# Load tiles of a cached attention kernel: fixed slots for K and V in place of a rotation of three

## The chip, the cores and the metric

The kernel runs on one core of a Trainium2 chip. The metric is device time in microseconds (us), the median over several executions. "Before" is the kernel as it was, "after" the changed one. Engines in the profile: PE is TensorE, PEld its weight loads, DVE is VectorE, ACT is ScalarE, SP is SyncE, and a q behind a name is that engine's sequencer, which issues the DMAs here. DMAs are the transfers that bring data from HBM, the memory in which the inputs lie, into the tiles on the core; the profile counts 16 DMA engines.

## The reference

Two independent attention blocks A and B are computed and their outputs set side by side. Each has 8 sequences of one token, 32 heads, a cache of 4096 keys and values of 128 elements, all in bfloat16.

```python
q = (x @ wq).reshape(B, Sq, H, Dh).transpose(0, 2, 1, 3)     # x: 8 x 1 x 1024
scores = einsum("bhqd,bhkd->bhqk", q, k_cache) * Dh ** -0.5  # k_cache: 8 x 32 x 4096 x 128
p = softmax(scores)
o = einsum("bhqk,bhkd->bhqd", p, v_cache)
out = o.transpose(0, 2, 1, 3).reshape(B, Sq, H * Dh) @ wo    # per block; the two are concatenated
```

Every byte of K and V is used once, so the kernel has to read 1.1 GB and does little with each byte.

## The kernel before

The caches are cut into 64 K tiles and 64 V tiles, each 8 heads of one sequence: 128 partitions of 64 KB, 8.39 MB. Three such tiles fit. They live in `ring`, in three slots taken in turn by everything that is loaded: wq, K, V, wo and the last part of wo (wo8).

```python
order = [("wq", 0), ("k", 0)]
for n in range(NQ):                      # NQ = 64
    if n == 0:
        order += [("wq", c) for c in range(1, NC)]
    if n + 1 < NQ:
        order.append(("k", n + 1))
    for c in range(NC):
        if n == done_at(c, NC, HB, B) + 1:   # n = 32 and 56
            order.append(("wo", c))
            late[n] = c
    if n == NQ - 1:
        order.append(("wo8", 0))
    order.append(("v", n))
pos = {kn: i for i, kn in enumerate(order)}

def tile_of(kind, n):
    return ring[:, pos[(kind, n)] % NSLOT, :]        # NSLOT = 3

def load_tiles():
    while issued[0] < len(order):
        i = issued[0]
        dep = op_xT if i == 2 else None
        if i >= NSLOT:
            dep = opUse.get(order[i - NSLOT])        # last use of the slot's tenant
            if dep is None:
                return
        ...                                          # one DMA, issued by SyncE behind dep
```

In the rotation V(n) takes the slot of K(n), and K(n+2), which comes next, that of V(n-1). The work on a K tile goes in 8 chunks: VectorE multiplies by q (L299), folds once (L304), TensorE adds up (L313), VectorE reduces (L321). `opUse[("k", n)]` is the TensorE step of the last chunk, `opUse[("v", n)]` the end of PV(n), the product with V(n). PV(n) is done in two halves of 32 matmuls, at chunks 5 and 6 of K tile n+1.

Of the kernel before, what the change touches and what calls it, by code (L numbers as in the profile page):

```python
# [31 lines left out]
class _Program:  # L32
# [9 lines left out]
    def add(self, eng, emit, deps=(), dma_key=None):  # L42
        op = _Op(eng, emit, list(deps), dma_key)
        if dma_key is not None:
            self.counts[dma_key] = self.counts.get(dma_key, 0) + 16
            op.token = (dma_key, self.counts[dma_key])
        for d in op.deps:
            if not (d.eng == "pe" and eng == "pe"):
                d.sig = True
        self.ops[eng].append(op)  # L50
        return op
# [38 lines left out]
def _build_kernel(nc, caches, out):  # L90
    B, Sq, D = caches[0][0].shape
    _, H, Sk, Dh = caches[0][1].shape
    NC = len(caches)
# [6 lines left out]
    CT = 32  # L100
    NR = T // CT
    HB = H // HQ
    NB = NC * HB
    NQ = NB * B
    NS = NQ * NR
    NSLOT = 3
    RG = T // 4 // 4
# [6 lines left out]
    with es:  # L114
# [4 lines left out]
        ring = sb("ring", [128, NSLOT, T * Dh], BF16)  # L119
# [31 lines left out]
        misc_bf16 = misc.bitcast(BF16)  # L151

        sems = {e: es.enter_context(nc.semaphore(f"c_{e}")) for e in ENGINES[1:]}
        for name, n in (("t", NSLOT), ("kl", 2), ("vl", 4), ("x", 1), ("out", 1)):
            for i in range(n):
                sems[(name, i)] = es.enter_context(nc.semaphore(f"{name}{i}"))

# [3 lines left out]
        def dma(out_ap, in_ap, key, deps, eng="sp"):  # L161
            return add(eng, lambda e: e.dma_start(out_ap, in_ap), deps, dma_key=key)  # L162
# [31 lines left out]
        outs = []  # L194


        order = [("wq", 0), ("k", 0)]
        late = {}
        for n in range(NQ):
            if n == 0:  # L200
                order += [("wq", c) for c in range(1, NC)]
            if n + 1 < NQ:
                order.append(("k", n + 1))

            for c in range(NC):
                if n == done_at(c, NC, HB, B) + 1:
                    order.append(("wo", c))
                    late[n] = c
            if n == NQ - 1:
                order.append(("wo8", 0))  # L210
            order.append(("v", n))
        pos = {kn: i for i, kn in enumerate(order)}
        issued = [0]

        def tile_of(kind, n):
            return ring[:, pos[(kind, n)] % NSLOT, :]

        def wo_rows(c):
            return MB * (HB if c < NC - 1 else HB - 1)

        def load_tiles():
            while issued[0] < len(order):
                i = issued[0]
                dep = op_xT if i == 2 else None
                if i >= NSLOT:
                    dep = opUse.get(order[i - NSLOT])
                    if dep is None:
                        return
                kind, n = order[i]
                to = tile_of(kind, n)  # L230
                key = ("t", i % NSLOT)
                if kind in ("k", "v"):
                    blk, b = divmod(n, B)
                    c, hb = divmod(blk, HB)
                    from_ = caches[c][1 if kind == "k" else 2][b, hb * HQ:(hb + 1) * HQ].rearrange("u (m t) d -> (u m) (t d)", m=MP)
                    cuts = [0, NR]
                    if n == NQ - 1:
                        cuts = [0, NR // 2, NR] if kind == "k" else [0, NR // 2, 3 * NR // 4, 7 * NR // 8, NR]
                    for g in range(len(cuts) - 1):
                        cols = slice(cuts[g] * CT * Dh, cuts[g + 1] * CT * Dh)  # L240
                        op = dma(to[:, cols], from_[:, cols], key if len(cuts) == 2 else (kind + "l", g), [dep])
                        for r in range(cuts[g], cuts[g + 1]):
                            opT[(kind, n, r)] = op
                elif kind == "wq":
                    opT[(kind, n)] = dma(to[:, 0:DC * H * Dh], caches[n][3].rearrange("(p k) n -> p (k n)", k=DC), key, [dep])
                elif kind == "wo":
                    rows = wo_rows(n)
                    opT[(kind, n)] = dma(to[0:rows, 0:H * D], caches[n][4][0:rows * H, :].rearrange("(p r) n -> p (r n)", r=H),
                                         key, [dep])
                else:  # L250
                    opT[(kind, n)] = dma(to[:, 0:HQ * D].rearrange("p (j n) -> p j n", j=HQ),
                                         caches[-1][4][(H - HQ) * Dh:, :].rearrange("(j p) n -> p j n", p=128), key, [dep])
                issued[0] += 1
# [91 lines left out]
        def make_pv(n, g0, g1):  # L345
            v = tile_of("v", n)

            def emit(e):
                for g in range(g0, g1):
                    for q in range(4):  # L350
                        t = 4 * (4 * g + q)
                        i = e.matmul(pv_ps[32 * q:32 * (q + 1), :], PM[:, t:t + 4, :].rearrange("p t j -> p (t j)"),  # L352
                                     v[:, t * Dh:(t + 4) * Dh], start=(g == 0), stop=(g == RG - 1), tile_position=(0, 32 * q))
                return i
            op = add("pe", emit, [opExp[n], opT[("v", n, g1 * NR // RG - 1)]] + _at(opAcc, n - 1, []))
            if g1 == RG:
                opPV[n] = opUse[("v", n)] = op

        def make_acc(n):
            opAcc[n] = [add("act", lambda e: e.activation(accS[:], pv_ps[:], ACTF.Copy), [opPV[n], _at(opExt, n - 1)])]  # L360
# [67 lines left out]

        def make_proj_last(norm):
            w = tile_of("wo8", 0)  # L430
            alone = ("wo", NC - 1) not in pos

            def emit(e):
                for j in range(HQ):
                    for q in range(NT):
                        x = e.matmul(proj[32 * q:32 * q + B, 0:DT], on8[:, j, :], w[:, j * D + q * DT:j * D + (q + 1) * DT],
                                     start=(alone and j == 0), stop=(j == HQ - 1), tile_position=(0, 32 * q))
                return x
            make_out(NC - 1, add("pe", emit, [norm, opT[("wo8", 0)], c_proj] + outs))
# [9 lines left out]
        one = sb("one", [128, 1], FP32)  # L449
        c_ones = one[:, 0:1]  # L450
        c_one = add("dve", lambda e: e.memset(one[:], 1.0))
        op_x = [dma(x_sb[:, c, :], caches[c][0].rearrange("b s d -> b (s d)"), ("x", 0), []) for c in range(NC)]

        def emit_xT(e):
            for c in range(NC):
# [2 lines left out]
                    i = e.transpose(misc_bf16[:, col:col + B], x_sb[:, c, :].rearrange("b (p k) -> b k p", k=DC)[:, k, :],  # L458
                                    ident[0:B, 0:B])
            return i  # L460
        op_xT = add("pe", emit_xT, [c_ident, op_x[-1]])
        load_tiles()
        c_xT = last["misc"] = add("dve", lambda e: e.tensor_copy(xT[:], misc_bf16[:, 0:NC * DC * B]), [op_xT])
        for hb in range(HB):
# [10 lines left out]
        for s in range(NS):  # L475
            n, r = divmod(s, NR)
            make_mul(s)
            if s >= 1:
                make_red(s - 1)
            if r == 0 and n >= 1:  # L480
                make_shift(n - 1)
            fold = make_fold(s)
            for k in range(4):
                v = pv_at.get(divmod(s - k, NR))
                if v is None:
                    continue

                k += v in late
                if k == 1 and v in late:
                    make_pv(v, 0, RG // 2)  # L490
                if k < 2:
                    make_pv(v, k * RG // 2, (k + 1) * RG // 2)
                if k == 1:
                    make_acc(v)
                if k == 2:
                    make_ext(v)
                if k == 3:
                    for c in range(NC):
                        if v == done_at(c, NC, HB, B):
                            make_norm(c)  # L500
            if r == 0 and n >= 1:
                make_exp(n - 1)
            if r == 2 and n % B == 0 and n >= 1:
                make_lsum(n // B - 1)

            if n == 0 and r >= 5:
                for i, (hb, f) in enumerate((hb, f) for hb in range(HB) for f in range(2)):
                    if i % 3 == r - 5:
                        for c in range(1, NC):
                            make_q(c, hb, f)  # L510
            c, hb = divmod(n // B, HB)
            if r == 2 and n % B == B - 1 and c + 1 < NC:
                make_qs(c + 1, hb, 0)
                make_qs(c + 1, hb, 1)
            if r == 3 and n + 1 < NQ:
                make_qbc(n + 1)
            if r >= 5 and n - 1 in late:
                i = r - 5
                make_proj(late[n - 1], i * H // 3, (i + 1) * H // 3)
            make_eacc(s, fold)  # L520
            load_tiles()


# [10 lines left out]
            on8[:].rearrange("p j b -> p b j"), o8_ps[:, 0:64].rearrange("p (b j) -> p b j", b=B),  # L534
            rl8[:].rearrange("p (b j) -> p b j", b=B), ALU.mult), [opLsum["rl"], opExt[n]])
        make_proj_last(norm)
        assert issued[0] == len(order)

        counts = P.tokens()
        for o in op_x:  # L540
# [57 lines left out]
```

## Time and profile before

| | before |
|---|---|
| time, median of 4 | 2636.54 us (2633.14 to 2640.33) |
| read from HBM | 1107.33 MB |
| rate over the span | 420 GB/s |
| load queue's packet time, share of 16 engines' span | 98.8% |
| VectorE busy | 80% |

The page's own lines on the queues, before (packets, MB, share of 16 engines; then the total):

```profile
q1 hardware_dynamic: 20688, 1107.35, 98.8%
HBM read 1107.33 MB, written 0.03 MB: 420 GB/s over the span
```

The windows view, before, in long stretches. The columns are the stretch, its length, busy time and instructions of each engine, the granted TensorE clock, the DMA share and GB/s:

```profile
500.00:1000.00 500.00, 244.25 (x1557) 72.57 (x1556) 413.42 (x356) 134.08 (x232) 0.00 (x0) 0.59 1.00 426
1500.00:2000.00 500.00, 244.06 (x1574) 73.12 (x1572) 415.68 (x358) 129.63 (x224) 0.00 (x0) 0.60 1.00 428
```

The last two columns show a share of 1.00 and a steady 426 to 428 GB/s (427 from 41 to 2287 us).

The timeline of the SyncE queue and, below it, of the VectorE steps that waited for a K tile, before (start, length, what; in brackets the idle time before it):

```profile
512.34 0.33 SPq L162 DMA_DIRECT2D ring<-in_A_v_cache_dram  x1
512.71 0.43 SPq L162 DMA_DIRECT2D ring<-in_A_k_cache_dram  x1
550.59 0.33 SPq L162 DMA_DIRECT2D ring<-in_A_v_cache_dram  x1
550.96 0.43 SPq L162 DMA_DIRECT2D ring<-in_A_k_cache_dram  x1
...
515.80 2.29 DVE L299 TENSOR_TENSOR ring<-ring,qbc 128x4096 bf16<-128x4096 bf16 x1 [5.44 <-DMA ring<-in_A_k_cache_dram]
555.29 2.29 DVE L299 TENSOR_TENSOR ring<-ring,qbc 128x4096 bf16<-128x4096 bf16 x1 [6.68 <-DMA ring<-in_A_k_cache_dram]
```

V and K are issued as a pair, and 3.5 us (512.34 to 515.80) and 4.7 us before VectorE starts on the K tile that is still in flight. One pair takes 555.29 - 515.80 = 39.5 us.

The waits view of the SyncE queue from 500 to 1000 us, before: it always waits for the score matmuls on K (13 pairs in 500 us).

```profile
SPq L162 <- PE red L313: 498.7, 13, 39.5
```

The DMA view, before: issues of each kind and the median us from issue to landing.

```profile
ring<-in_A_k_cache_dram SPq DMA_DIRECT2D x32, 43.3
ring<-in_A_v_cache_dram SPq DMA_DIRECT2D x32, 24.2
ring<-in_B_wo_dram SPq DMA_DIRECT2D x1, 33.0
```

And the end of the run, before, in windows of 4 us:

```profile
2592.00:2596.00 4.00, 3.96 (x34) 1.41 (x35) 1.45 (x1) 0.00 (x0) 0.00 (x0) 0.51 1.01 391
2596.00:2600.00 4.00, 3.74 (x44) 1.48 (x42) 3.19 (x3) 0.60 (x1) 0.00 (x0) 1.00 0.09 32
2600.00:2604.00 4.00, 1.37 (x4) 0.41 (x4) 2.57 (x3) 0.00 (x0) 0.00 (x0) 0.85 0.00 0
2604.00:2608.00 4.00, 0.41 (x1) 0.00 (x0) 1.79 (x5) 1.59 (x3) 0.00 (x0) 0.50 0.76 262
```

The last V is to take the last K's slot, so nothing is loaded while VectorE finishes that K. The chain of waits, before, ends with that load (start, us, what):

```profile
2605.77 20.62 DMA ring<-in_B_v_cache_dram
2626.43 1.07 PE pv L352 x8
```

### The profile page before, as it was taken

To read this page: it belongs to the slowest core of one execution; us is meant where nothing else is said; L and a number is where in the kernel's file an instruction comes from. 1 tells how busy PE (TensorE), PEld (TensorE's weight loads), DVE (VectorE), ACT (ScalarE), POOL (GpSimd) and SP (SyncE) were. 2 spreads that over 40 slices of the span, in tenths; PEclk is the share of its full clock that TensorE was granted. 3 is DMA by queue.
4 is the path that set the end of the run, shared out by engine and by line. 5 is a ranking of instruction groups with operands and counts; after the bars stand their busy time and mean duration, and the time that the engine had idled before them with its cause. 6 is when DMAs were issued, how large, how long until landed. Compare 5 with 4: busy or idle time off the path is not lost.

```text
span 2633.7 us, 19575 instructions
## 1 busy us (share of the span) xinstructions
PE 1256.2 (48%) x8130; PEld 380.7 (14%) x8130; DVE 2100.2 (80%) x1807; ACT 675.4 (26%) x1169; POOL 5.7 (0%) x23
## 2 busy tenths in 40 slices
PE   4554454454454454454453544544544544533454
PEld 1111111111111111111111111111111111111111
DVE  3788788888888888788885888888887887858885
ACT  0223223223223223223312232232232232213223
POOL 0000000000000000000000000000000000000000
PEclk8665665665665665665666656656656656665665
DMA  9999999999999999999999999999999999999997
GB/s 415 430 430 426 428 420 429 429 429 424 415 433 425 428 429 416 427 430 421 430 428 429 432 418 434 431 425 430 432 429 427 418 428 430 420 330 431 428 421 303
DMA packets 20840, 1108.61 MB, mean 421 GB/s; under 512 B 2272, under 2 KB 2336, under 8 KB 3376
## 3 DMA queue, kind: packets, MB, share of 16 engines
q1 hardware_dynamic: 20688, 1107.35, 98.8%
q8 instruction: 63, 1.03, 0.1%
q14 instruction: 25, 0.20, 0.0%
q10 hardware_dynamic: 64, 0.02, 0.0%
HBM read 1107.33 MB, written 0.03 MB: 420 GB/s over the span
## 4 chain that ended last, share of the span: by engine, by line
DMA 55%; DVE 36%; PE 6%; ACT 1%; issue 1%; SPq 0%; DVEq 0%
DMA ring<-in_A_k_cache_dram 26%; DMA ring<-in_B_k_cache_dram 25%; DVE ring L299 19%; DVE ring L304 10%; DVE s_sb L321 5%; PE red L313 4%; PE pv L352 2%; DMA ring<-in_B_v_cache_dram 2%; DMA ring<-in_B_wo_dram 1%; ACT PM L340 1%; DMA ring<-in_A_wq_dram 1%; PE q L263 1%; DVE rmax L327 1%; SPq L162 0%; DVE rtmp L329 0%
## 5 line engine op out<-in xcount | busy, mean ns | idle before, releaser
L299 DVE TENSOR_TENSOR ring<-ring,qbc 128x4096 bf16<-128x4096 bf16 x512 | 1170.1, 2285 | 464.8 <-DMA ring<-in_A_k_cache_dram 234.8
L313 PE MATMUL red<-ring,ident 128*128 128x512 bf16 x2048 | 845.8, 559 | 1293.7 <-DVE ring L304 1290.9
L340 ACT ACTIVATE PM<-s_sb,bias,own_sc 128x256 bf16<-128x256 f32 x512 | 609.3, 1607 | 894.6 <-DVE bias L333 894.6
L304 DVE TENSOR_TENSOR ring<-ring 128x2048 bf16<-128x2048 bf16 x512 | 622.0, 1215 | 0.0
L313 PEld LDWEIGHTS red<-ring,ident 128*128 128x128 bf16 x2048 | 203.8, 121 | 1840.7 <-DVE ring L304 1567.5
L321 DVE TENSOR_REDUCE s_sb<-red 128x32 f32<-128x512 f32 x512 | 349.9, 683 | 30.8 <-PE red L313 30.6
L352 PE MATMUL pv<-ring,PM 128*32 128x512 bf16 x4096 | 326.4, 475 | 21.1 <-DMA ring<-in_B_v_cache_dram 21.1
L360 ACT ACTIVATE accS<-pv 128x512 bf16<-128x512 f32 x64 | 38.2, 597 | 885.9 <-PE pv L352 885.9
L340 ACT ACTIVATION_READ_ACCUMULATOR PM<-s_sb,bias,own_sc 128x1 f32 x512 | 255.6, 499 | 0.0
L352 PEld LDWEIGHTS pv<-ring,PM 128*32 128x32 bf16 x4096 | 115.0, 115 | 239.0 <-issue 186.0
L289 ACT ACTIVATE qbc<-misc 128x128 bf16<-128x128 f32 x64 | 17.8, 277 | 138.5 <-PE misc L284 138.5
L263 PE MATMUL q<-ring,xT 128*8 128x512 bf16 x128 | 25.9, 411 | 19.6 <-DMA ring<-in_A_wq_dram 19.6
L373 PE MATMUL o<-accS,E 128*32 128x32 bf16 x896 | 31.7, 177 | 0.0
L373 PEld LDWEIGHTS o<-accS,E 128*32 128x32 bf16 x896 | 25.9, 94 | 24.2 <-ACT accS L360 14.0
L327 DVE TENSOR_REDUCE rmax<-s_sb 128x1 f32<-128x256 f32 x64 | 26.9, 420 | 2.2
L284 PE MATMUL misc<-q_sb,selb 8*32 8x128 bf16 x512 | 26.2, 295 | 0.8 <-ACT q_sb L272 0.8
L272 ACT ACTIVATE q_sb<-q 8x512 bf16<-8x512 f32 x16 | 9.3, 604 | 32.9 <-PE q L263 32.8
L329 DVE TENSOR_SCALAR rtmp<-half,rmax 128x32 f32<-128x32 f32 x64 | 15.4, 241 | 2.3
L284 PEld LDWEIGHTS misc<-q_sb,selb 8*32 8x32 bf16 x512 | 9.2, 103 | 53.9 <-issue 53.9
L333 DVE SCALAR_TENSOR_TENSOR bias<-own_sc,ngm,own_b 128x8 f32<-128x8 f32 x64 | 14.5, 226 | 2.3
L391 PE MATMUL o<-rsum,own_m 128*32 128x8 f32 x112 | 7.2, 202 | 18.2 <-ACT PM L340 18.2
L332 DVE TRANSPOSE_TENSOR_REDUCE ngm<-rtmp 128x1 f32<-128x32 f32 x64 | 13.5, 211 | 2.2
(37 smaller groups left out, 57.7 us busy)
## 6 DMA issues: line engine op xcount, KB each, us to landing
ring<-in_B_k_cache_dram SPq DMA_DIRECT2D x2, 4096.0 KB, 38.0
ring<-in_B_v_cache_dram SPq DMA_DIRECT2D x1, 4096.0 KB, 12.1
ring<-in_B_wo_dram SPq DMA_DIRECT2D x1, 2048.0 KB, 29.0
ring<-in_B_v_cache_dram SPq DMA_DIRECT2D x1, 2048.0 KB, 16.6
ring<-in_B_v_cache_dram SPq DMA_DIRECT2D x2, 1024.0 KB, 19.6
ring<-in_A_k_cache_dram SPq DMA_DIRECT2D x32, 43.3
ring<-in_A_v_cache_dram SPq DMA_DIRECT2D x32, 24.2
ring<-in_B_k_cache_dram SPq DMA_DIRECT2D x31, 43.3
```

Source lines behind the costliest of these rows:

```text
L263: i = e.matmul(q_ps[f][rows, :], xT[:, (c * DC + k) * B:(c * DC + k + 1) * B], w[:, col:col + 512], start=(k == 0), stop=(k == DC - 1), ti ...
L284: x = e.matmul(misc[32 * g:32 * (g + 1), 0:Dh], selb[rows, b, i, :], q_sb[rows, j * Dh:(j + 1) * Dh], start=(i == 0), stop=(i == 1), tile_ ...
L289: "act", lambda e: e.activation(qbc[:, n % 2, :], misc[:, 0:Dh], ACTF.Copy),
L299: opMul[s] = add("dve", lambda e: e.tensor_tensor(v, v, qbc[:, n % 2, :].unsqueeze(1).to_broadcast([128, CT, Dh]), ALU.mult), [opT[("k", n ...
L304: return add("dve", lambda e: e.tensor_tensor(v[:, :, 0:64], v[:, :, 0:64], v[:, :, 64:128], ALU.add), [opMul[s]])
L313: i = e.matmul(dst, ident[:], v[:, :, j, :], start=(j == 0), stop=(j == 3))
L321: opRed[s] = add("dve", lambda e: e.tensor_reduce(s_sb[:, n % 2, r * CT:(r + 1) * CT], red_ps[s % 2][:, :].rearrange("p (t w) -> p t w", w ...
L327: opRmax[n] = add("dve", lambda e: e.tensor_reduce(rmax[:], s_sb[:, n % 2, :], AX.X, ALU.max), [opRed[NR * n + NR - 1]])
L340: return e.activation(PM[:, :, j], s_sb[:, n % 2, :], ACTF.Exp, bias=bias[:, n % 2, j:j + 1], scale=own_sc[:, j:j + 1], accum_out=rsum[:, ...
L352: i = e.matmul(pv_ps[32 * q:32 * (q + 1), :], PM[:, t:t + 4, :].rearrange("p t j -> p (t j)"), v[:, t * Dh:(t + 4) * Dh], start=(g == 0), ...
L360: opAcc[n] = [add("act", lambda e: e.activation(accS[:], pv_ps[:], ACTF.Copy), [opPV[n], _at(opExt, n - 1)])]
L373: x = e.matmul(o_ps[MB * hb:MB * (hb + 1), H * b:H * (b + 1)], E[:, i, PH - 1 - u:PH - 1 - u + MB], accS[:, i * 128 + H * u:i * 128 + H * ...
```

## The change

K tiles take slots 0 and 1 in turn, V always takes slot 2, so V(n) waits for PV(n-1) and K(n+2) for K(n). PV is done in one block of 64 matmuls at chunk 5. x is loaded from ScalarE's queue. Half of the last V goes into a K slot ahead of wo8, the rest behind it.

```diff
-        order = [("wq", 0), ("k", 0)]
+        def put(kind, n, where=None, cuts=None):
+            if where is None:
+                where = kslot[0]
+                kslot[0] = 1 - where
+            slot[(kind, n)] = where
+            plan.append((kind, n, cuts))
+        put("wq", 0, 1)
+        put("k", 0)
+        put("wq", 1, 2)
+        for n in range(NQ - 1):
+            if n + 2 < NQ:
+                put("k", n + 1)
+            else:
+                put("k", n + 1, cuts=((0, NR // 2), (NR // 2, NR)))
             for c in range(NC):
                 if n == done_at(c, NC, HB, B) + 1:
-                    order.append(("wo", c))
+                    put("wo", c)
                     late[n] = c
-            if n == NQ - 1:
-                order.append(("wo8", 0))
-            order.append(("v", n))
+            put("v", n, 2)
+        put("v", NQ - 1, cuts=((0, NR // 2),))
+        put("wo8", 0, 2)
+        plan.append(("v", NQ - 1, ((NR // 2, 3 * NR // 4), (3 * NR // 4, 7 * NR // 8), (7 * NR // 8, NR))))
... # tile_of and load_tiles go by slot[] and by the slot's tenant before
-        op_x = [dma(x_sb[:, c, :], ..., ("x", 0), []) for c in range(NC)]
+        op_x = [dma(x_sb[:, c, :], ..., ("x", 0), [], "act") for c in range(NC)]
... # PV of tile v, at chunk 5 + k of the next K tile
-                if k < 2:
-                    make_pv(v, k * RG // 2, (k + 1) * RG // 2)
-                if k == 1:
-                    make_acc(v)
+                if k == 0:
+                    make_pv(v, 0, RG)
+                    make_acc(v)
```

More of the change, by code (lines that the diff above doesn't have):

```diff
@@ L153, in _build_kernel @@
         sems = {e: es.enter_context(nc.semaphore(f"c_{e}")) for e in ENGINES[1:]}
-        for name, n in (("t", NSLOT), ("kl", 2), ("vl", 4), ("x", 1), ("out", 1)):
+        for name, n in (("t", NSLOT), ("kl", NR), ("vl", NR), ("x", 1), ("out", 1)):
             for i in range(n):
@@ L194, in _build_kernel @@
         outs = []
-        order = [("wq", 0), ("k", 0)]
+        plan = []
+        slot = {}
         late = {}
-        for n in range(NQ):
-            if n == 0:
-                order += [("wq", c) for c in range(1, NC)]
-            if n + 1 < NQ:
-                order.append(("k", n + 1))
+        kslot = [0]
+        def put(kind, n, where=None, cuts=None):
[12 more added lines that the diff above has]
+                put("k", n + 1, cuts=((0, NR // 2), (NR // 2, NR)))
             for c in range(NC):
                 if n == done_at(c, NC, HB, B) + 1:
-                    order.append(("wo", c))
+                    put("wo", c)
                     late[n] = c
-            if n == NQ - 1:
-                order.append(("wo8", 0))
-            order.append(("v", n))
-        pos = {kn: i for i, kn in enumerate(order)}
+            put("v", n, 2)
+        put("v", NQ - 1, cuts=((0, NR // 2),))
+        put("wo8", 0, 2)
+        plan.append(("v", NQ - 1, ((NR // 2, 3 * NR // 4), (3 * NR // 4, 7 * NR // 8), (7 * NR // 8, NR))))
+        tenant = [None, None, ("x", 0)]
+        before = []
+        for kind, n, cuts in plan:
+            w = slot[(kind, n)]
+            before.append(tenant[w])
+            tenant[w] = (kind, n)
         issued = [0]
         def tile_of(kind, n):
-            return ring[:, pos[(kind, n)] % NSLOT, :]
+            return ring[:, slot[(kind, n)], :]
         def wo_rows(c):
@@ L221, in load_tiles @@
         def load_tiles():
-            while issued[0] < len(order):
-                i = issued[0]
-                dep = op_xT if i == 2 else None
-                if i >= NSLOT:
-                    dep = opUse.get(order[i - NSLOT])
+            while issued[0] < len(plan):
+                kind, n, cuts = plan[issued[0]]
+                prev = before[issued[0]]
+                dep = None
+                if prev not in (None, (kind, n)):
+                    dep = opUse.get(prev)
                     if dep is None:
                         return
-                kind, n = order[i]
                 to = tile_of(kind, n)
-                key = ("t", i % NSLOT)
+                key = ("t", slot[(kind, n)])
                 if kind in ("k", "v"):
@@ L235, in load_tiles @@
                     from_ = caches[c][1 if kind == "k" else 2][b, hb * HQ:(hb + 1) * HQ].rearrange("u (m t) d -> (u m) (t d)", m=MP)
-                    cuts = [0, NR]
-                    if n == NQ - 1:
-                        cuts = [0, NR // 2, NR] if kind == "k" else [0, NR // 2, 3 * NR // 4, 7 * NR // 8, NR]
-                    for g in range(len(cuts) - 1):
-                        cols = slice(cuts[g] * CT * Dh, cuts[g + 1] * CT * Dh)
-                        op = dma(to[:, cols], from_[:, cols], key if len(cuts) == 2 else (kind + "l", g), [dep])
-                        for r in range(cuts[g], cuts[g + 1]):
+                    for r0, r1 in cuts or ((0, NR),):
+                        cols = slice(r0 * CT * Dh, r1 * CT * Dh)
+                        op = dma(to[:, cols], from_[:, cols], (kind + "l", r0) if cuts else key, [dep])
+                        for r in range(r0, r1):
                             opT[(kind, n, r)] = op
@@ L430, in make_proj_last @@
             w = tile_of("wo8", 0)
-            alone = ("wo", NC - 1) not in pos
+            alone = ("wo", NC - 1) not in slot
             def emit(e):
@@ L451, in _build_kernel @@
         c_one = add("dve", lambda e: e.memset(one[:], 1.0))
-        op_x = [dma(x_sb[:, c, :], caches[c][0].rearrange("b s d -> b (s d)"), ("x", 0), []) for c in range(NC)]
+        op_x = [dma(x_sb[:, c, :], caches[c][0].rearrange("b s d -> b (s d)"), ("x", 0), [], "act") for c in range(NC)]
         def emit_xT(e):
@@ L460, in emit_xT @@
             return i
-        op_xT = add("pe", emit_xT, [c_ident, op_x[-1]])
+        op_xT = opUse[("x", 0)] = add("pe", emit_xT, [c_ident, op_x[-1]])
         load_tiles()
@@ L482, in _build_kernel @@
             fold = make_fold(s)
-            for k in range(4):
+            for k in range(3):
                 v = pv_at.get(divmod(s - k, NR))
@@ L486, in _build_kernel @@
                     continue
-                k += v in late
-                if k == 1 and v in late:
-                    make_pv(v, 0, RG // 2)
-                if k < 2:
-                    make_pv(v, k * RG // 2, (k + 1) * RG // 2)
+                if k == 0:
+                    make_pv(v, 0, RG)
+                    make_acc(v)
                 if k == 1:
-                    make_acc(v)
+                    make_ext(v)
                 if k == 2:
-                    make_ext(v)
-                if k == 3:
                     for c in range(NC):
@@ L536, in _build_kernel @@
         make_proj_last(norm)
-        assert issued[0] == len(order)
+        assert issued[0] == len(plan)
         counts = P.tokens()
```

## The prediction

> **What bounds it now.** The DMA engines. The page gives the load queue 98.8% of the 16 engines' span and 1107.33 MB read at 420 GB/s, against 80% for VectorE. In the windows view the stretch 41 to 2287 us runs at 427 GB/s, DMA share 1.00. The Trainium skill (HBM Reference, section Access) states about 425 GB/s for a core streaming alone; this trace agrees. One tile (8.39 MB) costs 19.7 us, a K+V pair 39.4 us. VectorE needs about 33.5 us per K tile (8 x (2.29+0.60+1.13) plus 1.2), so it waits for K: 465 us over 63 waits.
>
> Three places aren't at full rate. (a) B's wo load (96 partitions): 33.0 us for 6.3 MB, about 18 us over its share. The change keeps this transfer. (b) The last V: the timeline issues it at 2604.4, when the last K is used, because it rotates into that slot; the 4 us windows show DMA at 32, 0 and 262 GB/s from 2596 to 2608, a hole of 9 to 10 us. It lands at 2626.4. (c) The start: two x issues (0.37+0.28 us) precede the first weight load at 1.56 us.
>
> **What the change does.**
> - Steady state: today V(n) and K(n+2) are issued together when K(n) is used, about 4 us before the tile in flight lands (K's 43.3 us from issue to landing minus 39.4). After, V(n) is issued when PV(n-1) ends, some 13 us before the queue would run dry, and K some 20 us before. With the share already 1.00 this hides little: 0 to 8 us, central 2.
> - PV in one block of 64 matmuls (3.5 us for the first 32, about 6 us together): VectorE waits about 2 us more per tile, inside the 5 to 7 us that it waits for DMA anyhow. No cost until the tail.
> - x on ScalarE's queue: minus 0.7 us. The skill (DMA: Bandwidth & Descriptors, section Issuing engines are not separate DMA queues) says this saves issue time only.
> - Tail: half of the last V goes into K62's slot behind V62, then wo8, then the rest; the hole closes and the last V lands about 2616. But the last K's score work doesn't move: VectorE runs without a gap from 2533.6 on, the exponentials end at 2615.9 today and 2 us later with the longer PV block. The whole last PV (6 us) follows, ending near 2623.5 instead of 2627.5. Of 10 us gained by DMA about 4 reach the end: the bound passes to VectorE and ScalarE.
>
> Sum: 0.7 + 4 + 2, about 7 us (0.25%). **Predicted 2630 us, 2618 to 2637 (8 in 10).** Chances: faster by over 2% 0.01, within 2% 0.98, slower 0.01.
>
> **What would show it.** Mid-run windows still at 425 to 430 GB/s; K's median issue to landing up from 43.3 to about 60 us, V's from 24.2 to about 30 (queued longer, not slower); SyncE's waits split between score matmuls and PV; no DMA hole before the end; the chain of waits in the tail through VectorE and the exponentials, not the last V load; the 330 GB/s slice at B's wo stays.
>
> **What would make it wrong.** If the 16 engines finish a tile unevenly, the shallow queue lets fast ones idle and 427 GB/s isn't the ceiling: a deeper queue could give 15 to 20 us. If V comes later than chunk 5 of the next tile, the longer PV block holds score work, and VectorE could become the bound. If B's wo load was slow because of its neighbours, its 18 us could change too.

## The result, and the profile after

| | before | after |
|---|---|---|
| median of 4 | 2636.54 us | 2604.84 us (2603.57 to 2605.85) |
| ratio | | 0.9879 (95% interval 0.9862 to 0.9896) |
| rate over the span | 420 GB/s | 425 GB/s |
| load queue's share | 98.8% | 99.1% |

Here and below a ratio is the mean time of one kernel's runs over that of the other's of the same rounds, so not quite the ratio of the medians quoted. 31.7 us is clear of noise and over four times the 7 us predicted.

The page's queue lines, after:

```profile
q1 hardware_dynamic: 20656, 1107.32, 99.1%
HBM read 1107.33 MB, written 0.03 MB: 425 GB/s over the span
```

The windows view, after, in the same stretches as before:

```profile
500.00:1000.00 500.00, 239.19 (x1529) 72.80 (x1526) 420.39 (x361) 137.33 (x238) 0.00 (x0) 0.60 1.00 433
1500.00:2000.00 500.00, 248.34 (x1588) 75.54 (x1586) 421.04 (x361) 135.21 (x234) 0.00 (x0) 0.60 1.00 433
```

The DMA share still reads 1.00, and the rate is 433 GB/s in place of 426 to 428. So at a share of 1.00 the engines were not moving all they could.

The timeline of the SyncE queue and of VectorE's waits for K, after:

```profile
500.15 0.33 SPq L162 DMA_DIRECT2D ring<-in_A_v_cache_dram  x1
508.84 0.33 SPq L162 DMA_DIRECT2D ring<-in_A_k_cache_dram  x1
538.29 0.33 SPq L162 DMA_DIRECT2D ring<-in_A_v_cache_dram  x1
546.98 0.33 SPq L162 DMA_DIRECT2D ring<-in_A_k_cache_dram  x1
...
510.61 2.29 DVE L315 TENSOR_TENSOR ring<-ring,qbc 128x4096 bf16<-128x4096 bf16 x1 [3.74 <-DMA ring<-in_A_k_cache_dram]
549.32 2.29 DVE L315 TENSOR_TENSOR ring<-ring,qbc 128x4096 bf16<-128x4096 bf16 x1 [4.31 <-DMA ring<-in_A_k_cache_dram]
```

V is now issued 10.5 us (500.15 to 510.61) before VectorE starts on the K in flight, and K apart from it. A pair takes 549.32 - 510.61 = 38.7 us, 0.8 us less than the pair shown of before. The waits of the SyncE queue from 500 to 1000 us are now split:

```profile
SPq L162 <- PE pv L368: 389.6, 13, 32.5
SPq L162 <- PE red L329: 106.7, 13, 8.3
```

The DMA view, after: V is queued 6 us longer, K is not.

```profile
ring<-in_A_k_cache_dram SPq DMA_DIRECT2D x32, 41.3
ring<-in_A_v_cache_dram SPq DMA_DIRECT2D x32, 30.3
ring<-in_B_wo_dram SPq DMA_DIRECT2D x1, 32.6
```

The tail, after, in windows of 4 us: no window before the last V has landed is empty.

```profile
2568.00:2572.00 4.00, 4.00 (x54) 1.72 (x47) 0.97 (x1) 0.19 (x1) 0.00 (x0) 0.73 1.01 430
2572.00:2576.00 4.00, 1.86 (x12) 0.68 (x10) 3.23 (x3) 0.41 (x1) 0.00 (x0) 1.00 0.79 286
2576.00:2580.00 4.00, 1.41 (x4) 0.43 (x4) 2.53 (x3) 0.00 (x0) 0.00 (x0) 0.62 1.10 412
```

The chain of waits at the end, after: the exponentials and the whole last PV, no longer a load.

```profile
2582.48 9.46 ACT PM L356 x16
2592.67 5.96 PE pv L368 x54
```

**Where the time came from.** In the profiled runs (2633.7 and 2604.0 us) B's wo has landed at 2337.5 before and 2313.1 after, so 24.4 of the 29.7 us were gained by then, in the steady part. From the arrival of the last K but one to the end it took 100.1 us before (from 2533.6) and 96.3 us after (from 2507.65): the tail gave 3.8 us.

The trace also holds every DMA packet. In the steady part a packet is one row of 64 KB, and the usual one takes 2.418 us; 16 engines at that pace move 16 x 65536 B / 2.418 us = 433.6 GB/s. I went through the packets from 34 to 2229 us of the run, and for each V issue counted the bytes issued but not yet moved ("queued", in us at 433.6 GB/s; median and range are over the V issues ahead of tile 32). The third row is what the packets took beyond 2.418 us each; those over 2.45 us alone make up 24.1 us of it before and 4.0 us after:

```
                              before     after
packets in the stretch         14283     14453
packets over 2.45 us            1344       177
time over 2.418 us, per engine  25.5 us    6.9 us
engines idle, per engine        11.8 us    4.8 us
sum lost                        37.3 us   11.7 us
queued at V's issue, median      2.1 us    8.0 us   (before 0.5 to 3.9, after 6.2 to 9.6)
```

The difference of the sums, 25.6 us, is the gain of the steady part: the 170 packets that after moves more in the same stretch are worth 25.7 us at 2.418 us on 16 engines. The table says where the time went, not yet why. A slow packet counts as busy time, which is why the share read 1.00 throughout. Before, the loss follows the data queued when V was issued (slow packets plus idle engines, us per issue, over the issues in that stretch, less the one or two just behind wo): 1.70 below 0.5 us queued (1 issue), 0.93 at 0.5 to 1.5 us queued (12 issues), 0.61 at 1.5 to 2.5 (19), 0.18 at 2.5 to 3.5 (16), 0.07 at 3.5 to 5 (4). After, with 5 to 12 us queued, it is 0.05 to 0.06 (53 issues). A second count, over the 10 us from each issue on, gives 1.96, 0.96, 0.66, 0.18, 0.07 and 0.06 for the same classes.

### The profile page after: what moved, and what is told of

It reads as the page before. It is cut to its first block, busy times and chain, and to the rows that moved or that the text cites. A ratio compares the mean times of both kernels' runs of the same rounds, so it can differ in the third digit from the quotient of the medians. Undisturbed runs are those within 1.5% of the kernel's fastest.

```text
span 2604.0 us, 19575 instructions
## 1 busy us (share of the span) xinstructions
PE 1256.4 (48%) x8130; PEld 387.1 (15%) x8130; DVE 2103.5 (81%) x1807; ACT 675.6 (26%) x1169; POOL 5.7 (0%) x23
## 3 DMA queue, kind: packets, MB, share of 16 engines
q1 hardware_dynamic: 20656, 1107.32, 99.1%
## 4 chain that ended last, share of the span: by engine, by line
DMA 53%; DVE 32%; PE 13%; ACT 2%; issue 1%; DVEq 0%
DMA ring<-in_A_k_cache_dram 26%; DMA ring<-in_B_k_cache_dram 24%; DVE ring L315 16%; DVE ring L320 10%; PE pv L368 6%; PE red L329 6%; DVE s_sb L337 5%; ACT PM L356 1%; DMA ring<-in_B_wo_dram 1%; DMA ring<-in_B_v_cache_dram 1%; DMA ring<-in_A_wq_dram 1%; PE q L279 1%; DVE rmax L343 1%; DVE rtmp L345 0%; DVE bias L349 0%
## 5 line engine op out<-in xcount | busy, mean ns | idle before, releaser
L337 DVE TENSOR_REDUCE s_sb<-red 128x32 f32<-128x512 f32 x512 | 350.2, 684 | 126.1 <-PE red L329 126.1
L368 PE MATMUL pv<-ring,PM 128*32 128x512 bf16 x4096 | 318.0, 479 | 16.6 <-DMA ring<-in_B_v_cache_dram 16.6
L368 PEld LDWEIGHTS pv<-ring,PM 128*32 128x32 bf16 x4096 | 121.5, 118 | 233.7 <-issue 178.8
L389 PE MATMUL o<-accS,E 128*32 128x32 bf16 x896 | 31.7, 177 | 0.0
L389 PEld LDWEIGHTS o<-accS,E 128*32 128x32 bf16 x896 | 25.9, 94 | 24.2 <-ACT accS L376 23.3
## 6 DMA issues: line engine op xcount, KB each, us to landing
ring<-in_A_k_cache_dram SPq DMA_DIRECT2D x32, 41.3
ring<-in_A_v_cache_dram SPq DMA_DIRECT2D x32, 30.3
```

What stands on the lines that cost most here:

```text
L337: opRed[s] = add("dve", lambda e: e.tensor_reduce(s_sb[:, n % 2, r * CT:(r + 1) * CT], red_ps[s % 2][:, :].rearrange("p (t w) -> p t w", w ...
L368: i = e.matmul(pv_ps[32 * q:32 * (q + 1), :], PM[:, t:t + 4, :].rearrange("p t j -> p (t j)"), v[:, t * Dh:(t + 4) * Dh], start=(g == 0), ...
L389: x = e.matmul(o_ps[MB * hb:MB * (hb + 1), H * b:H * (b + 1)], E[:, i, PH - 1 - u:PH - 1 - u + MB], accS[:, i * 128 + H * u:i * 128 + H * ...
```

## The experiments

**Theory (reserve):** the change pays because V is issued earlier. More data stand in the queue when the tile in flight runs out, so no engine slows down or runs dry at the change of tiles. **Rivals:** the fixed slots themselves, the single PV block, x or the tail brought the gain; or it is that two DMAs are no longer issued at the same moment.

### late_v: the change with V issued late again

```diff
+                deps = [dep]
+                if kind == "v" and 1 <= n < NQ - 3:
+                    if ("k", n) not in opUse:
+                        return
+                    deps.append(opUse[("k", n)])
-   op = dma(..., [dep])
+   op = dma(..., deps)
```

> The changed kernel, but every V in mid-run also waits until the K tile of the same number is used, so V and the next K are issued together, as before the change; slots, x queue, PV block and tail stay changed. Reserve theory (the data still queued when the next tile is issued sets the rate): mid-run falls back to 424 to 427 GB/s, packets over 2.45 us are again over 1000, time 2625 to 2640 us. Rival (fixed slots, the single PV block, x or the tail brought the gain): stays at 431 to 433 GB/s and 2600 to 2608 us.

Measured: 2661.1 us, ratio 1.0098 to before (1.0082 to 1.0114). The windows view of late_v, and the timeline of its SyncE queue:

```profile
500.00:1000.00 500.00, 233.94 (x1553) 71.49 (x1554) 410.69 (x354) 128.68 (x224) 0.00 (x0) 0.61 0.99 424
```

```profile
514.78 0.33 SPq L162 DMA_DIRECT2D ring<-in_A_v_cache_dram  x1
515.15 0.43 SPq L162 DMA_DIRECT2D ring<-in_A_k_cache_dram  x1
```

With nothing altered but the moment of V's issue, the whole gain is lost and more. The size was missed: I expected 2625 to 2640. The packets say why it is worse than before: with the longer PV block a K tile is used up 36.3 us after VectorE starts on it in place of 34.9 (medians), so a median of 0.7 us is queued in place of 2.1, and the engines idle 34.0 us (before 11.8) besides 26.7 us of slow packets (here and below the third row of the table). The rivals "slots", "PV block", "x" and "tail" all stayed in this kernel and did not save it.

### late_v_apart: late, but V and K not issued together

```diff
+                if kind == "k" and 3 <= n < NQ - 3:
+                    if NR * (n - 1) not in opEacc:
+                        return
+                    deps.append(opEacc[NR * (n - 1)])
```

> As late_v, and every K in mid-run also waits for the first chunk of the K tile before it, so it is issued some 6 us after V, alone, with 15 us of data still queued. If the shallow reserve at V's issue is what costs: no better than late_v (within 4 us). If it is the burst of two issues at once that slows the packets: most of late_v's loss is gone, 2600 to 2612 us.

Measured: 2654.53 us, ratio 1.0075 (1.0059 to 1.0092). The timeline shows the two issues apart:

```profile
516.41 0.33 SPq L162 DMA_DIRECT2D ring<-in_A_v_cache_dram  x1
529.75 0.33 SPq L162 DMA_DIRECT2D ring<-in_A_k_cache_dram  x1
```

The medians differ by 6.6 us, a little more than the 4 us I allowed, of the 56 us that late_v stands above after. Slow packets cost 27.5 us and idle engines 29.2 us, nearly as in late_v. So the pair of issues is at most a small part, and the shallow reserve nearly all of it. (K came a median of 9.9 us after V, with 11.3 us queued; I had expected 6 and 15.)

These two runs also sharpen the count by reserve. Over the 10 us from V's issue on they lose 1.69 and 1.63 us below 0.5 us queued (14 and 12 issues), 1.29 and 1.22 at 0.5 to 1.5 us (16 and 18), but only 0.07 and 0.09 at 2 to 3.5 us (21 each), where before still loses 0.34 (25 issues). So below about 2 us the loss follows the reserve in all three kernels. Why before loses more than these two at 2 to 3.5 us is open.

### rot_half: the rotation kept, V's first half loaded early

This is the kernel before. Only V is loaded in two halves, the first as soon as the first four chunks of the K tile in its slot are used, with a semaphore of its own.

```diff
+    if kind == "v" and 0 < n < NQ - 1 and order[i - NSLOT] == ("k", n):
+        if (i, 0) not in half_op:
+            if NR * n + NR // 2 - 1 not in opEacc:
+                return
+            ...
+            half_op[(i, 0)] = dma(tile_of(kind, n)[:, cols], from_[:, cols], ("ha", i % NSLOT),
+                                  [opEacc[NR * n + NR // 2 - 1]])
...
-                    cuts = [0, NR]
+                    cuts = [NR // 2, NR] if split else [0, NR]
```

> The kernel before with its rotation of three slots, x, halves of PV and tail as they were; only each V is loaded as two halves, the first as soon as the first four chunks of the K tile in its slot are used. That gives about 18 us of queued data at V's first issue, and the second half and the next K are still issued together. Reserve theory: 431 to 433 GB/s in mid-run and 24 us less than before, 2608 to 2616 us. If fixed slots matter in themselves, or the burst of issues: stays near 2636 us.

Measured: 2610.13 us, ratio 0.9904 (0.9887 to 0.9920). The windows view and the timeline of rot_half (x2 are the two halves of V, merged; the second is issued together with K):

```profile
500.00:1000.00 500.00, 238.52 (x1553) 71.96 (x1552) 417.11 (x359) 137.34 (x238) 0.00 (x0) 0.60 1.00 432
```

```profile
530.72 15.22 SPq L162 DMA_DIRECT2D ring<-in_A_v_cache_dram  x2
545.98 0.43 SPq L162 DMA_DIRECT2D ring<-in_A_k_cache_dram  x1
```

With the old slots, the old PV halves, the old x and the old tail, 26 of the 32 us are there. About 16.6 us (median) are queued at V's first half, and 10.8 us at the second, which goes out together with K: a pair of issues costs little when enough is queued. This and late_v are the two sides of the proof: with the rotation kept the gain comes, with the fixed slots kept it goes. What decides is how early the load goes out; the number of slots was three throughout and was not tested.

### pv_halves: the change with PV in two halves

```diff
-            for k in range(3):
+            for k in range(4):
...
-                if k == 0:
-                    make_pv(v, 0, RG)
-                    make_acc(v)
+                k += v in late
+                if k == 1 and v in late:
+                    make_pv(v, 0, RG // 2)
+                if k < 2:
+                    make_pv(v, k * RG // 2, (k + 1) * RG // 2)
+                if k == 1:
+                    make_acc(v)
```

> The changed kernel with PV in two halves of 32 matmuls again, a chunk apart, so V is issued about 4 us later, with some 4 to 5 us of queued data in place of 8 to 9. Reserve theory with a threshold near 3.5 us (the trace of before loses nothing where 3 us or more were queued): 2602 to 2608 us, VectorE's wait for the score matmuls back to about 30 us of 126. If one PV block was itself worth the gain: slower by over 10 us.

Measured: 2603.98 us, ratio 0.9878 (0.9863 to 0.9893), the same as after (0.9879). A median of 7.1 us is queued (4.5 at the least), and it loses no more than after. So the single block is worth nothing in time; its cost, 126.1 us of VectorE's waits for the score matmuls in place of 31.5, lies in time that VectorE would spend waiting for K.

### x_sync and last_v_own: two parts of the change undone

```diff
-        op_x = [dma(..., ("x", 0), [], "act") for c in range(NC)]
+        op_x = [dma(..., ("x", 0), []) for c in range(NC)]
```

> The changed kernel with x on SyncE's queue again. The first weight load is issued 0.75 us later and everything behind it with it: 0.5 to 1.5 us slower, seen in the time of the first K issue after the projection of q rather than in the total. If x from ScalarE's queue costs (its packets now land among the weights'): as fast or faster.

Measured: 2606.0 us, ratio 0.9892 (0.9874 to 0.9911), which can't be told from after. The chain of waits shows the first K that waits for the projection of q issued at the same time; first after, then x_sync:

```profile
38.56 43.39 DMA ring<-in_A_k_cache_dram
```

```profile
38.55 44.06 DMA ring<-in_A_k_cache_dram
```

The equal times are a coincidence. The weights land at 22.96 us in after and at 23.60 in x_sync, and the projection starts at 23.10 and 23.73, so x does move its start by 0.6 us. But its first matmuls take 631 to 634 ns each until some moment and 379 ns from then on: until 27.2 us in after, 26.5 in x_sync and 29.1 before. In each of the three the profile's first record of the granted clock starts at that moment. What sets the moment, the runs do not show; it came earlier in x_sync and cancelled the 0.6 us, and it came later before, where the first K was issued at 39.76. So this sign can't test x, and the total can't tell 0.7 us from noise.

```diff
-        put("v", NQ - 1, cuts=((0, NR // 2),))
-        put("wo8", 0, 2)
+        put("wo8", 0)
+        put("v", NQ - 1, 2, cuts=((0, NR // 2),))
```

> The changed kernel with the last V in V's own slot, behind V62, and wo8 in the K slot: the part of the change named last, undone. The last V then is issued when PV62 ends, lands some 4 to 6 us later, but PV63 waits for the exponentials until about 2592 anyhow: 0 to 3 us slower, 2604 to 2608 us. If the last V load bounds the tail: 5 us slower or more.

Measured: 2607.16 us, ratio 0.9896 (0.9878 to 0.9915). The difference to after is within the noise between the two sets of rounds. The tail needs only that the last V does not wait for the last K; V's own slot gives that too.

### v_first: V ahead of wo

After has a new hole before each wo: V stands in the queue behind wo, which waits for a K tile. The windows view, after, around A's wo (tile 32):

```profile
1315.00:1320.00 5.00, 3.58 (x57) 1.59 (x50) 3.94 (x4) 0.60 (x1) 0.00 (x0) 1.00 0.84 357
1320.00:1325.00 5.00, 2.10 (x8) 0.51 (x6) 4.97 (x5) 0.00 (x0) 0.00 (x0) 0.93 0.54 236
```

```diff
-                    put("wo", c)
                     late[n] = c
             put("v", n, 2)
+            if n in late:
+                put("wo", late[n])
...
-        pv_at = {((n + 2, 0) if n in late else (n + 1, 5)): n for n in range(NQ - 1)}
+        pv_at = {(n + 1, 5): n for n in range(NQ - 1)}
...
-            if r >= 5 and n - 1 in late:
-                i = r - 5
-                make_proj(late[n - 1], i * H // 3, (i + 1) * H // 3)
+            if r == 0 and n - 2 in late:
+                make_proj(late[n - 2], 0, H)
```

> The changed kernel, with V issued ahead of wo where both fall together (tiles 32 and 56), PV of that tile at its usual chunk, and the projection in one go at the start of the tile two later. In the changed kernel V stands behind wo, which waits for a K tile to be used, and the queue runs dry at both places (147 and 262 GB/s in one 4 us window each). Reserve theory: both holes close, 3 to 4 us each, 2595 to 2601 us. If the holes have another cause, or the projection block now holds up score work: 2603 us or more.

Measured: 2610.01 us, ratio 0.9907 (0.9886 to 0.9929): a miss, some 5 us slower than after by the medians, though the two intervals overlap a little. The first hole is gone, but one as large opened behind wo, where the next K waits for a K tile and nothing else is queued (v_first, windows view):

```profile
1355.00:1360.00 5.00, 2.15 (x23) 0.87 (x21) 4.35 (x4) 0.30 (x1) 0.00 (x0) 0.92 0.69 292
1360.00:1365.00 5.00, 1.89 (x4) 0.43 (x4) 1.41 (x2) 0.00 (x0) 0.00 (x0) 0.50 0.79 301
```

At B's wo the slow stretch also grew: 137 packets of over 3 us in place of 109.

### v_first_wo128, wo128: B's wo on all partitions

B's wo is loaded into 96 partitions. In the packets of after, 93 in its stretch take over 4 us (median 5.0) in place of 2.418. A's wo, which has all 128 partitions, lands 22.2 us after its issue in the same run.

```diff
-                    rows = wo_rows(n)
+                    rows = MB * HB          # 128; the rows past 96 are loaded and not used
```

> As v_first, and B's wo loaded on all 128 partitions (2.1 MB more, the rows of the last head block not used) in place of 96. If the 96-partition shape is what makes it slow (about 193 GB/s): 8.4 MB at 433 GB/s take 19.4 us in place of 32.6, so 12 to 13 us less than v_first. If its neighbours in the queue made it slow: no gain, or 5 us more.

> The changed kernel, with B's wo loaded on 128 partitions and nothing else altered. v_first lost 5 us to the changed kernel and v_first_wo128 gained 17 us on v_first. If the 96-partition shape alone is slow: 12 to 13 us less than the changed kernel, about 2592 us, with no slice near 320 GB/s. If part of the 17 us came from how wo's slow packets meet the tiles behind them: less than 10 us here.

Measured: v_first_wo128 2593.39 us, ratio 0.9844 (0.9826 to 0.9862); wo128, the same edit on the changed kernel itself, 2595.63 us, ratio 0.9839 (0.9822 to 0.9855). The windows view around B's wo, first after, then wo128:

```profile
2290.00:2310.00 20.00, 7.89 (x24) 1.88 (x24) 18.13 (x14) 4.95 (x11) 0.00 (x0) 0.50 0.98 210
```

```profile
2290.00:2310.00 20.00, 13.28 (x113) 4.63 (x114) 20.00 (x17) 4.92 (x11) 0.00 (x0) 0.56 0.97 419
```

Both show a share near 1, and one moves twice what the other does. The DMA view of wo128: B's wo lands 10.9 us sooner after its issue than the 32.6 us of after, though it is larger.

```profile
ring<-in_B_wo_dram SPq DMA_DIRECT2D x1, 21.7
```

Loading 2.1 MB more saves 9 us by the medians (12 to 13 expected); on top of v_first it saves 17, more than expected. In v_first 121 packets took over 4 us, more than the 96 rows of B's wo, so packets of the tiles around it were slow too.

### v_first_split_wo128: the second hole closed too

As v_first_wo128, and the K tile behind wo is loaded as two halves, the first when half of the K tile in its slot is used.

```diff
+            if n - 1 in late:
+                put("k", n + 1, cuts=((0, NR // 2),))
+                plan.append(("k", n + 1, ((NR // 2, NR),)))
-            if n + 2 < NQ:
+            elif n + 2 < NQ:
...
+                if kind == "k" and n - 2 in late:
+                    dep = opEacc.get(NR * (n - 1) + cuts[0][1] - 1)
+                    if dep is None:
+                        return
+                    prev = None
```

> As v_first_wo128, and the K tile issued behind wo is loaded as two halves, the first when half of the K tile in its slot is used. In v_first the hole only moved: from before wo to behind it, where the next K waits for a K tile to be used and nothing else is queued (292 and 301 GB/s in two 5 us windows). Reserve theory: that hole closes too, 3 to 4 us at each of two places, 2585 to 2590 us. If the hole isn't from the late issue: 2593 us.

Measured: 2593.88 us, ratio 0.9833 (0.9818 to 0.9847). The hole is closed (windows view of v_first_split_wo128):

```profile
1355.00:1360.00 5.00, 1.74 (x21) 0.77 (x20) 4.75 (x5) 0.00 (x0) 0.00 (x0) 1.00 0.99 423
1360.00:1365.00 5.00, 1.54 (x4) 0.36 (x4) 1.00 (x1) 0.00 (x0) 0.00 (x0) 0.65 1.02 439
```

But the total did not reach the 2585 to 2590 us expected, and its interval overlaps those of wo128 and v_first_wo128. Where the closed holes' time went is open. These three are the fastest kernels, 9 to 11 us below after and 41 to 43 us below before by their medians; which of them is best the runs don't tell.

## Why the prediction was wrong

- **What bounds it: half right.** DMA bounds the kernel before and after. The step that failed is "With the share already 1.00 this hides little: 0 to 8 us, central 2". The steady part gave 24.4 us, and the mid-run windows, foretold at "425 to 430 GB/s", read 433. The share counts the time that packets take, slow ones too, so it reads 1.00 at 427 and at 433 GB/s. The Trainium skill (Perfetto Trace Analysis, section Identifying the Most-Contended Engine) says to judge DMA by bytes moved against the peak and not by occupancy; this trace agrees, most plainly with wo at a share of 0.98 and 210 GB/s. The peak could have been had from the trace of before: most of its packets, too, take 2.418 us, which is 433.6 GB/s. I took the 425 GB/s of the skill (HBM Reference; it stands in section Specifications (TRN2), not in Access as the prediction has it) for a confirmation that 427 was the ceiling, which it could not be: these runs hold 433.
- **The reserve: mis-sized.** I put it at "about 4 us", from 43.3 us minus 39.4. But 39.4 us is the pair's time with the losses in it; at 433.6 GB/s it is 38.7. And issue to landing also holds the delays of start and landing: the run's first packet starts 1.0 us after its issue in the packet records. (K's 41.3 us after are 19 us queued, 19.3 of its own and so some 3 us of such delays.) The median of what was really queued was 2.1 us. After, it was 8.0 and not "some 13". My prediction named the right way to be wrong ("the shallow queue lets fast ones idle ... a deeper queue could give 15 to 20 us"), but kept the range above it.
- **K's wait in the queue: wrong.** "up from 43.3 to about 60 us" was 41.3: K is issued, as before, behind one V and little else (a median of 19 us queued, 21 before). The prediction's own "K some 20 us before" was right and, with 19.7 us for the tile itself, contradicts its 60. V's rise from 24.2 to about 30 was right (30.3).
- **PV in one block, no cost in steady state: right.** Shown by pv_halves.
- **x, 0.7 us: not decided.** In x_sync the projection starts 0.6 us later, but the total can't show it. **The tail, about 4 us: right** (3.8), and the end of the chain is the exponentials and the last PV, as foretold. The hole before the end is gone.
- **B's wo: kept, as foretold** (33.0 and 32.6 us). Not foretold were the new holes before wo, where V is held behind it.

So the sum failed in one term: 2 us for the steady part, where the trace shows 24.4.

What stays open: why packets in flight take longer when little is queued behind them (before, the 1344 slow ones took 0.29 us more than 2.418 on average). late_v_apart shows that it is not mainly the pair of issues; the mechanism in the queue is not shown. Open too are why 96 partitions load at half the rate, and where the time of the holes closed last went.

## What to carry to other kernels

This DMA-bound loop lost over 1% of its time (27 to 30 us of 2195 by the two counts) at the hand-overs between tiles while its busy share read 1.00: compare GB/s with the pace of the fastest common packet, and compute how much is still queued when the next load is issued. Tie a load to the earliest release there is (another slot's tenant, or half a tile), so that enough is queued at every issue, here some 4 us of data; which slots were used for it did not matter. A load on fewer partitions can be slower than a larger one on all of them: here 32.6 us on 96 and 21.7 on 128.

## What the Trainium skill lacked or had wrong

- DMA: Bandwidth & Descriptors says to issue a DMA early, but not how much must be queued to hold the full rate. Before, an issue with 0.5 to 1.5 us queued lost 0.93 us, with 2.5 to 3.5 us 0.18 us; after, with 5 us or more, 0.05 to 0.06 us.
- HBM Reference, section Specifications (TRN2), gives about 425 GB/s for a core streaming alone. These runs hold 431 to 433 GB/s over hundreds of us when the queue is kept deep, near the 435 GB/s that DMA: Bandwidth & Descriptors, section Where 436 GB/s comes from, states as the fabric's ceiling.
- Perfetto Trace Analysis calls DMA occupancy misleading, but not that slow packets hide in it: before, 1344 of 14283 packets in the steady part were slow at a share of 1.00.
- DMA: Bandwidth & Descriptors counts a 96-partition tile among those that run on all 16 engines. In this trace they are all busy (share 0.98), but the stretch of the load runs at 210 GB/s, and that of the load with 128 partitions at 419. SBUF — State Buffer, section Door 1: The DMA port swizzle, gives a table of the rate by partitions, without 96.
